# Seven-product output GEMM in the second MLP, and block 1's attention turned by TensorE, in a pooled-attention plus two-MLP kernel

## Chip, cores and metric

One core of one Trainium2 chip. The metric is the device time of one execution in microseconds (us). Before the change it is 1756.0 us, the median of three runs (1752.55 to 1757.51).

## What is computed

```python
def _attn_ref(q, k, v):                       # q, k, v: (8, 8, 576, 64)
    k_p = k.reshape(B, H, Sp, 8, D).mean(axis=3)
    v_p = v.reshape(B, H, Sp, 8, D).mean(axis=3)
    scores = scale * np.matmul(q, k_p.transpose(0, 1, 3, 2))
    scores = scores - np.max(scores, axis=-1, keepdims=True)
    attn = np.exp(scores)
    attn = attn / (np.sum(attn, axis=-1, keepdims=True) + 1e-09)
    return np.matmul(attn, v_p)

def _moe_ref(x, w_in, w_out):                 # (4608, 512) -> 2048 -> 512
    h = x @ w_in
    g = np.where(h >= 1, h, np.where(h <= -1, 0.0, (h + 1) ** 2 / 4))
    return g @ w_out

def _moe2_ref(x, w_gate, w_val, w_out):       # (4608, 512) -> 1536 -> 512
    gate = 1.0 / (1.0 + np.exp(-(x @ w_gate)))
    return (gate * (x @ w_val)) @ w_out
```

The attention's output, turned to 4608 tokens by 512, goes through the first MLP and its result through the second. All arrays are fp32.

## The kernel before

The 4608 tokens are nine blocks of 512 (`TB`). Every fp32 product of the MLPs is made of three matmuls of rounded parts: `three` (L578) multiplies high by high, high by low and low by high. So an operand has to be split first: ScalarE rounds it to its high part, VectorE subtracts that and leaves the low part (`split2`, L698; `split_to`, L704; `high_part` and `low_part`, L502 and L512).

**Attention.** `unit` (L363) does two heads of one block: load the queries, turn them, multiply with the pooled keys, exponentials and sums, turn the exponentials, multiply with the pooled values. There are 36 of them, four per block; those of block j + 1 run beside the first MLP of block j. Block 0 is turned by TensorE (`first`, L364: transposes at L384 and L447, a copy out of PSUM after each). All other blocks are turned by VectorE's stream transposes of 32 x 32 pieces: the queries at L401, loaded in pieces of 32 x 32 by eight SP transfers per unit at L395, and the exponentials at L458, which then need twelve SP transfers `aT<-aq` per unit (L464) that put the pieces in place.

**First MLP.** For each block and each of 16 column groups, `columns` (L584) makes `h<-x,win`, ScalarE and VectorE the activation and its split, and four groups of `acc<-g,wj` add up the output. The weights `w_in` and `w_out` are loaded as the first block needs them (`weight`, L527; loads at L543 and L547) and converted by ScalarE and VectorE (L551 to L565). The weights of the second MLP are loaded meanwhile, and their converted form kept in DRAM.

**Second MLP.** Block 0 is done plainly, while `prepare` (L730) builds the sums of gate and value weights that Strassen's method (in Winograd's form) wants, splits them and stores them in DRAM (`seven`, 12 tensors of 1.79 MB). Blocks 1 to 8 go in four pairs. For each pair, each of six steps `i` and for gate and value, seven products (`product`, L882) of six matmuls each take the place of eight: the 2 x 2 parts of the weights are multiplied with the inputs of two blocks and their sums (`T1` to `T4`). Their results are combined by VectorE's additions (`add`, L890) and one ScalarE copy of a bank to SBUF (L917), then `finish` (L897) makes sigmoid and product. The out GEMM is plain: `out_part` (L779) splits the activations `gs` and makes `acc<-win,g`, 144 matmuls per block, with the output weights held in SBUF; `out_rows` (L592) copies four banks out and stores them.

**What sets the order.** `Plan` (L66 to L193) is a list scheduler that runs while the program is built. Each operation has an engine, a cost and a due time (`key`); `issue` takes for the engine that is free first the operation whose data and buffers are ready, with the smallest key. Each engine then works through its list in order, and so does SP's queue of transfers. The keys around the change are:

```python
T0, S1, S2 = START, STEP1, 7.8
def due1(s): return T0 + S1 * s
def due2(j, m): return due1(NB * M1 + 2) + S2 * (j * M2 + m)
PSTEP = 11 * 2.6
PAIR0 = due2(1, 0) + 1
T0p = PAIR0 + PSTEP * MP * pr                 # start of pair pr; MP = 6 steps
T = T0p + PSTEP * i + PSTEP / 2 * n           # n: gate or value
```

PSUM has eight banks: four `acc`, two `h`, two `a`. A pair's products use `h` and `a`, its out GEMM `acc`.

Of the kernel before, what the change touches and what calls it, by code (L numbers as in the profile page):

```python
# [18 lines left out]
P = 128  # L19
# [45 lines left out]
class Plan:  # L65
# [7 lines left out]
    def op(self, eng, cost, key, fn, r=(), w=(), after=(), behind=(), nbytes=0, share=1.0, dmas=1):  # L73
# [24 lines left out]
        o.data, o.order = data, order - data  # L98
# [98 lines left out]
def pooled_attention_two_mlps(  # L197
# [46 lines left out]
    one, att, two = ExitStack(), ExitStack(), ExitStack()  # L244
# [118 lines left out]
    def unit(j, p, T):  # L363
        h0, first = 2 * p, j == 0  # L364
# [9 lines left out]
        if first:  # L374

            qs = buf_a("q", 2, [P, NT4, 2, D])
            for h in range(2):
                op(SP, 0.475, T - 20, lambda h=h: nc.sync.dma_start(
                    out=qs.t[:, :, h], in_=q[0, h0 + h, 0:TB].rearrange("(s t) d -> s t d", t=NT4)), w=[qs], nbytes=TB * D * 8)
            ptq = bank("acc")  # L380

            def transposes():
                for t in range(NT4):
                    nc.tensor.transpose(out=ptq.t[:, P * t:P * t + P],  # L384
                                        in_=qs.t[:, t].rearrange("s h d -> s (h d)"), identity=ident.t)
# [18 lines left out]
        e = buf_g(F32, (P, NT4, 2, P)) if first else e_sb  # L404
        sums = buf_a("sm", 2, [P, NT4, 2])

        scs = [bank("h" if first and p % 2 else "a") for _ in range(2)]
# [31 lines left out]
        if first:  # L439

            flat = Src(aT, lambda t: t.rearrange("c a h t j -> c (a h t j)"))
            for h in range(2):
                pt = bank("acc")

                def transposes(h=h, pt=pt):
                    for t in range(NT4):
                        nc.tensor.transpose(out=pt.t[:C].rearrange("c (s t) -> c t s", t=NT4)[:, t], in_=e.t[:, t, h, 0:C], identity=ident.t)  # L447
# [21 lines left out]
        px, x = bank("acc" if first else "a"), buf_x()  # L469

        def values():
            for t0, n, b, s0 in segs:

                cuts = sorted({t0, t0 + n} | {c for c in (-(-t0 // P) * P, (t0 + n) // P * P) if t0 < c < t0 + n})
                for lo, hi in zip(cuts, cuts[1:]):
                    for h in range(2):
                        at = aT.t[:, :, h].rearrange("c a t j -> c t a j")
                        if first:
                            rhs = flat()[:, TB * h:TB * h + TB]
# [7 lines left out]
        op(PE, 0.86 + 0.25 * (len(segs) > 1 and j % 2), T + 18 - AHEAD_PX * first, values,  # L487
           r=[aT] + [vps[b % 2, p] for _, _, b, _ in segs], w=[px], share=C / P)
        op((ACT, DVE), (0.48, 0.6), T + 19 - AHEAD_PX * first, (
# [3 lines left out]
        op(DVE, 0.6, T + 19 - AHEAD_PX * first, lambda: nc.vector.scalar_tensor_tensor(  # L493
# [175 lines left out]

    pools2 = {}  # L670

    def second_a():
        att.close()
        pools2["wa"] = two.enter_context(tc.tile_pool(name="wa", bufs=2))

    def second_b():
        one.close()
        pools2["right"] = two.enter_context(tc.tile_pool(name="two", bufs=1, side="right"))

    open_a = op("none", 0.0, 0.0, second_a, behind=att_ops)  # L680
    open_b = op("none", 0.0, 0.0, second_b, behind=one_ops)

    def late(tag, bufs, shape, dtype=F32, fifo=True):

        b = Buf(lambda: pools2["wa" if tag == "wa" else "right"], tag, bufs, shape, dtype, fifo)
        b.behind = [open_a if tag == "wa" else open_b]
# [6 lines left out]
    def buf_win(behind):  # L693
        b = Buf(win_p, "win", M1, [P, 2, TB], F32R)
# [14 lines left out]
    PSTEP = 11 * 2.6  # L709
# [55 lines left out]
    def load_seven(n, i, key):  # L765
        sl, d = buf_seven(), seven[2 * i + n]
        op2(SP, 0.475, key, lambda: nc.sync.dma_start(
            out=sl.t.rearrange("p s k f -> p (s k f)").bitcast(F32), in_=d.t), r=[d], w=[sl], nbytes=P * 2 * NMAT * HK * 4)
        return sl
# [9 lines left out]
    def out_part(gs, m, key, accs, last, ahead=5):  # L779
        g = buf_g()  # L780
        op2(ACT, 0.62, key - ahead, lambda: nc.scalar.copy(out=g.t[:, 0], in_=gs.t), r=[gs], w=[g])  # L781
        op2(DVE, 0.69, key - ahead + 1, lambda: nc.vector.tensor_tensor(  # L782
            out=g.t[:, 1], in0=gs.t, in1=g.t[:, 0].bitcast(F32), op=ALU.subtract), r=[gs, g], w=[g])
# [6 lines left out]

    def buf_gs():
        return late("gs", 12, [P, TB], fifo=False)
# [9 lines left out]
    accs = [bank("acc") for _ in range(4)]  # L802
# [167 lines left out]
```

## Time and profile before

| | us |
|---|---|
| median of three runs | 1756.0 |
| lowest, highest | 1752.55, 1757.51 |
| the profiled execution, its own time | 1755.67 |
| its span | 1753.8 |
| TensorE (PE) busy | 1723.8 (98%) |
| VectorE (DVE) busy | 1051.5 (60%) |
| ScalarE (ACT) busy | 805.7 (46%) |
| GpSimd (POOL) busy | 52.7 (3%) |

The profile is one execution. The span runs from its first to its last instruction; the time of the execution is 1.9 us longer. TensorE's granted clock was 0.995 of full speed over the span. A matmul's duration in the rows includes its way through the array, so the cost of one among many is read from the distance of two starts. Line numbers in rows are those of the kernel before; from L384 on the changed kernel's lines are five higher (`three` is L585 to L587 there), and more from L667 on.

### The profile page before, as it was taken

Reading aid. Unit: us, or ns where it says so; the run is one execution under the profiler, and the core shown is the slowest. Engines: PE = TensorE matmul, PEld = TensorE weight load, DVE = VectorE, ACT = ScalarE, POOL = GpSimd, SP = SyncE. Lnnn points to the kernel's source line nnn. Section 1 sums busy time; section 2 is a strip of 40 time slices with the busy share of each in tenths; the row PEclk is TensorE's granted clock in tenths of the full one; section 3 lists DMA queues with packets and bytes.
Section 4 is the critical chain, followed back from the end, with each engine's and each line's share of the span. In section 5 each row is a group of like instructions: output and inputs, shape, how many; then the busy total and the mean of one; then the engine's idle time right before and its main releaser. Section 6 shows DMA issues by size and latency. Waiting matters only on the chain.

```text
span 1753.8 us, 24039 instructions
## 1 busy us (share of the span) xinstructions
PE 1723.8 (98%) x9016; PEld 1393.4 (79%) x9016; DVE 1051.5 (60%) x1874; ACT 805.7 (46%) x1786; POOL 52.7 (3%) x90
## 2 busy tenths in 40 slices
PE   7899999999999999999999999999999999999998
PEld 5676777778777778777887888888888888888887
DVE  5899867677776867574646645345444644464432
ACT  5876656566665656564755332123222312141212
POOL 0000001010010101010000000000000000000000
PEclk9999999999999999999999999999999999999999
DMA  7742525243443414031415875354344433443411
GB/s 205 229 119 69 149 57 163 62 134 97 116 116 92 134 45 134 16 128 40 174 39 202 318 291 204 126 192 145 126 146 166 149 119 146 166 167 126 150 43 49
DMA packets 148532, 234.37 MB, mean 134 GB/s; under 512 B 84160, under 2 KB 104640, under 8 KB 140736
## 3 DMA queue, kind: packets, MB, share of 16 engines
q1 hardware_dynamic: 138624, 182.50, 33.1%
q0 software_dynamic: 9792, 50.34, 7.9%
q8 instruction: 71, 1.16, 0.3%
q14 instruction: 45, 0.37, 0.1%
HBM read 173.02 MB, written 50.33 MB: 127 GB/s over the span
## 4 chain that ended last, share of the span: by engine, by line
PE 92%; DMA 3%; DVE 2%; ACT 1%; SPq 0%; issue 0%; DVEq 0%; ACTq 0%
PE acc L580 13%; PE h L580 13%; PE acc L582 13%; PE acc L581 13%; PE h L582 13%; PE h L581 12%; PE a L582 4%; PE a L581 4%; PE a L580 4%; PE a L484 2%; DMA raw<-in_moe_w_out_dram 1%; PE a L413 1%; DMA kv<-in_v_dram 1%; DMA x<-in_v_dram 1%; DMA xb<-y 0%
## 5 line engine op out<-in xcount | busy, mean ns | idle before, releaser
L580 PE MATMUL h<-x,win 128*128 128x512 f32 x576 | 231.2, 401 | 1.0 <-ACT win L505 1.0
L580 PE MATMUL acc<-g,wj 128*128 128x512 f32 x576 | 228.7, 397 | 1.2 <-ACT g L505 1.2
L582 PE MATMUL acc<-g,wj 128*128 128x512 f32 x576 | 225.4, 391 | 3.5 <-DVE wj L514 3.5
L582 PE MATMUL h<-x,win 128*128 128x512 f32 x576 | 225.7, 392 | 1.3 <-DVE win L514 1.3
L581 PE MATMUL acc<-g,wj 128*128 128x512 f32 x576 | 225.6, 392 | 1.0 <-DVE g L514 1.0
L581 PE MATMUL h<-x,win 128*128 128x512 f32 x576 | 225.5, 391 | 0.0
L781 ACT CAST g<-gs 128x512 fp32r<-128x512 f32 x108 | 66.8, 622 | 319.2 <-PE acc L582 200.4
L645 ACT ACTIVATE t<-h,half 128x512 f32<-128x512 f32 x144 | 99.2, 689 | 186.9 <-PE h L582 186.9
L582 PE MATMUL acc<-win,g 128*128 128x512 f32 x432 | 168.2, 389 | 2.1 <-DVE g L782 2.1
L580 PE MATMUL acc<-win,g 128*128 128x512 f32 x432 | 168.2, 389 | 0.0
L581 PE MATMUL acc<-win,g 128*128 128x512 f32 x432 | 168.1, 389 | 0.0
L782 DVE TENSOR_TENSOR g<-gs,g 128x512 fp32r<-128x512 f32 x108 | 74.1, 690 | 135.2 <-ACT g L781 135.0
L649 DVE SCALAR_TENSOR_TENSOR t<-t,h 128x512 f32<-128x512 f32 x144 | 97.3, 676 | 90.9 <-ACT t L647 90.8
L580 PEld LDWEIGHTS h<-x,win 128*128 128x128 f32 x576 | 108.7, 189 | 35.7 <-issue 9.7
L582 PEld LDWEIGHTS acc<-g,wj 128*128 128x128 f32 x576 | 108.4, 188 | 28.4 <-DVE wj L514 5.4
L580 PEld LDWEIGHTS acc<-g,wj 128*128 128x128 f32 x576 | 108.2, 188 | 27.8 <-ACT g L505 1.7
L582 PEld LDWEIGHTS h<-x,win 128*128 128x128 f32 x576 | 108.7, 189 | 25.9 <-DVE win L514 2.5
L581 PEld LDWEIGHTS acc<-g,wj 128*128 128x128 f32 x576 | 108.3, 188 | 23.2 <-DVE g L514 1.6
L581 PEld LDWEIGHTS h<-x,win 128*128 128x128 f32 x576 | 108.8, 189 | 21.1
L514 DVE TENSOR_TENSOR wj<-wout_f,wj 128x512 fp32r<-128x512 f32 x144 | 99.0, 688 | 33.3 <-ACT wj L505 33.0
L514 DVE TENSOR_TENSOR g<-t,g 128x512 fp32r<-128x512 f32 x144 | 98.8, 686 | 33.6 <-ACT g L505 33.1
L505 ACT CAST g<-t 128x512 fp32r<-128x512 f32 x144 | 89.1, 619 | 52.5 <-DVE t L649 50.1
(212 smaller groups left out, 3231.1 us busy)
## 6 DMA issues: line engine op xcount, KB each, us to landing
wa<-seven SPq DMA_DIRECT2D x32, 1792.0 KB
wb<-seven SPq DMA_DIRECT2D x16, 1792.0 KB
seven<-wa POOLq DMA_DIRECT2D x8, 1792.0 KB, 7.4
y<-raw SPq DMA_DIRECT2D x18, 512.0 KB
w<-f POOLq DMA_DIRECT2D x36, 256.0 KB, 2.5
out_dram<-raw SPq DMA_DIRECT2D x18, 512.0 KB
win<-in_moe_w_in_dram SPq DMA_DIRECT2D x16, 512.0 KB
raw<-in_moe_w_out_dram SPq DMA_DIRECT2D x16, 512.0 KB
```

The lines of the kernel that those rows point to most:

```text
L413: nc.tensor.matmul(out=scs[h].t[r0 % P:r0 % P + D, r0 // P * C:r0 // P * C + C], lhsT=qT.t[D * h:D * h + D, r0:r0 + D], rhs=kts[b % 2, p]. ...
L484: nc.tensor.matmul(out=px.t[D * h:D * h + D, lo:hi], lhsT=vps[b % 2, p].t[:, h], rhs=rhs, start=True, stop=True)
L505: ACT: (0.52, lambda: nc.scalar.copy(out=dst.t[:, 0], in_=src())),
L514: op(engs, [0.6 if e == DVE else 1.23 for e in engs], key, [lambda e=e: by[e].tensor_tensor(out=dst.t[:, 1], in0=src(), in1=dst.t[:, 0].bi ...
L580: nc.tensor.matmul(out=o, lhsT=wh, rhs=xh, start=start, stop=False, skip_group_check=more)
L581: nc.tensor.matmul(out=o, lhsT=wh, rhs=xl, start=False, stop=False, skip_group_check=more)
L582: nc.tensor.matmul(out=o, lhsT=wl, rhs=xh, start=False, stop=stop, skip_group_check=more)
L645: op(ACT, 0.69, Tg, lambda t=t, hps=hps: nc.scalar.activation(out=t.t, in_=hps.t, func=AF.Relu, bias=half.t, scale=0.5), r=[hps, half], w=[t])
L649: op(DVE, 0.69, Tg + 2, lambda t=t, hps=hps: nc.vector.scalar_tensor_tensor(out=t.t, in0=t.t, scalar=1.0, in1=hps.t, op0=ALU.min, op1=ALU. ...
L781: op2(ACT, 0.62, key - ahead, lambda: nc.scalar.copy(out=g.t[:, 0], in_=gs.t), r=[gs], w=[g])
L782: op2(DVE, 0.69, key - ahead + 1, lambda: nc.vector.tensor_tensor(out=g.t[:, 1], in0=gs.t, in1=g.t[:, 0].bitcast(F32), op=ALU.subtract), r ...
```

## The change

It has four parts.

1. **Block 1 is turned by TensorE too** (`first = j <= 1`). Its queries come in 16 transfers of 256-byte pieces and not 32 of 128-byte pieces, 16 transposes and 32 transposes of exponentials are added on TensorE with banks `a`, twelve copies out of PSUM follow (eleven on ScalarE, one on VectorE by the order), and twelve stream transposes and 48 transfers `aT<-aq` go.

2. **The out GEMM of a pair goes by seven products** (`out_pair`): seven products of six steps of two banks of three matmuls, 252 for 288. `prepare_out` builds and splits the sums of output weights in pair 0 and stores them in DRAM (42 tiles `seven_o`, by POOL); each product loads them again (`wo`, five buffers). The activations' sums are made in place by VectorE (24 per pair), each product's own split follows (42 per pair, 24 before). The output comes out transposed: `store` turns it by VectorE and stores 256-byte pieces, and the last part of the last pair goes through eight transposes of TensorE (`store_rows`).

3. **Gate and value products in another order**, with sums made in PSUM: ScalarE copies a finished bank into the next one (`to_bank`), and the next product adds to it. Weights come one product at a time (256 KB, `ws`, nine buffers) and not seven at a time (1.79 MB, three buffers).

4. **Input sums kept in DRAM** (`input_sums`): those of pairs 1 to 3 are made during the pair before, stored and loaded again; pair 0 makes its own as before.

Per engine the order counts 6912 matmuls of 512 columns by three parts after the change and 7056 before.

```diff
-        h0, first = 2 * p, j == 0
+        h0, first = 2 * p, j <= 1
...
+            where = "acc" if j == 0 else "a"
+            ptq = bank(where)
...
-                        out=pt.t[:C].rearrange("c (s t) -> c t s", t=NT4)[:, t], in_=e.t[:, t, h, 0:C], identity=ident.t)
+                        out=pt.t[:C, P * t:P * t + P], in_=e.t[:, t, h, 0:C], identity=ident.t)
...
-    PSTEP = 11 * 2.6
+    PSTEP = 10.5 * 2.6
...
-    def load_seven(n, i, key):
-        sl, d = buf_seven(), seven[2 * i + n]
+    def load_seven(n, i, mat, key):
+        w, d = late("ws", 9, [P, 2, HK], F32R), seven[2 * i + n]
...
+        for k in range(NMAT):
+            src, n = (a, (0, 2, 3)[k]) if k < 3 else (sm, k - 3)
+            w = buf_wo()
...
+            op2(PL, 1.0, key + 2 + k, lambda w=w, k=k: nc.gpsimd.dma_start(
+                out=seven_o[i][k].t, in_=w.t.rearrange("p s f -> p (s f)").bitcast(F32)), r=[w], w=[seven_o[i][k]], nbytes=P * 2 * HK * 4)
...
+        def product(n, mat, o, start, what):
+            chain = []
+            for i in range(MP):
+                key = K0 + KP * (n + i / MP)
+                w, g = late("ws", 9, [P, 2, HK], F32R) if last and n and i % 3 else buf_wo(), buf_g() if i % 2 else late("g2", 3, [P, 2, TB], F32R)
+                op2(SP, 0.475, key - 20, lambda w=w, i=i: nc.sync.dma_start(
+                    out=w.t.rearrange("p s f -> p (s f)").bitcast(F32), in_=seven_o[i][mat].t),
+                    r=[seven_o[i][mat]], w=[w], nbytes=P * 2 * HK * 4)
+                h1, h2 = hs[i]
+                src, b = what(key - 32, h1, h2)
+                split_to(key - 30, lambda src=src, b=b: src.t[:, b], lambda g=g: g.t[:, 0], lambda g=g: g.t[:, 1], 0.69, src, g)
+
+                def mm(w=w, g=g, i=i):
+                    for e in range(2):
+                        es = slice(e * P, e * P + P)
+                        three(o[e].t, w.t[:, 0, es], w.t[:, 1, es], g.t[:, 0], g.t[:, 1],
+                              start and i == 0, i == MP - 1, not start)
...
+        X, Y = [bank("acc", True) for _ in range(2)], [bank("acc", True) for _ in range(2)]
+        product(0, 0, X, True, lambda k, h1, h2: (h1, 0))
+        s1 = o_buf()
+        to_sbuf(key(1) - 30, X, s1)
...
+        if pr == 0:
...
+        else:
+            order = (("B11", B11), ("T1", T1), ("T2", T2), ("B21", B21), ("T3", T3), ("B22", B22), ("T4", T4))
+            for n, (name, x) in enumerate(order):
+                for kt in range(2):
...
+                    op2(SP, 0.475, key - AHX, lambda x=x, kt=kt, d=d, r0=r0: nc.sync.dma_start(
+                        out=x[kt].t[:, 1].bitcast(F32), in_=d.t[r0 * P:(r0 + 1) * P, :]), r=[d], w=[x[kt]], nbytes=P * TB * 4)
+                    x_split(x[kt], key)
...
+            if pr + 1 < NPR and i in (2, 4):
+                input_sums(pr + 1, i // 2 - 1, T0p + PSTEP * (i + SUM0), plan.ops[-1])
...
                 product(0, A, 0, B11, True)
-                op(ACT, 0.6, T + H * 1, lambda s1=s1, A=A: nc.scalar.copy(out=s1.t, in_=A.t), r=[A], w=[s1])
-                product(1, Bk, 4, T2, True)
-                add(T + H * 2, u2, Bk, s1)
-                product(2, Ck, 5, T3, True)
-                add(T + H * 3, u3, Ck, u2)
-                product(3, Dk, 3, T1, True)
-                finish(T + H * 4, (1, 1), Dk, u3)
-                product(4, A, 1, B21, False)
-                finish(T + H * 5, (0, 0), A, None)
-                product(5, Ck, 2, T4, False)
-                finish(T + H * 6, (1, 0), Ck, u2)
-                product(6, Dk, 6, B22, False)
-                finish(T + H * 7, (0, 1), Dk, u2)
+                to_bank(T + H * 1, A, Bk)
+                product(1, Dk, 3, T1, True)
+                op2(ACT, 0.6, T + H * 2 + 0.6, lambda u5=u5, Dk=Dk: nc.scalar.copy(out=u5.t, in_=Dk.t), r=[Dk], w=[u5])
+                product(2, Bk, 4, T2, False)
+                to_bank(T + H * 3, Bk, Ck)
+                op2(ACT, 0.6, T + H * 3 + 1, lambda u2=u2, Bk=Bk: nc.scalar.copy(out=u2.t, in_=Bk.t), r=[Bk], w=[u2])
+                product(3, A, 1, B21, False)
+                finish(T + H * 4, (0, 0), A, None)
+                product(4, Ck, 5, T3, False)
+                finish(T + H * 5, (1, 1), Ck, u5)
+                product(5, Dk, 6, B22, False)
+                finish(T + H * 6, (0, 1), Dk, u2)
+                product(6, Ck, 2, T4, False)
+                finish(T + H * 7, (1, 0), Ck, None)
```

SP's queue while block 0 is in the first MLP and block 1's attention runs, before (`q` are query pieces, `aT<-aq` the exponentials' pieces, `raw` a weight load):

```order
L313 DMA kv<-in_k_dram 72x2x512
L395 DMA q<-in_q_dram 32x2x32
L395 DMA q<-in_q_dram 32x14x32
L464 DMA aT<-aq 32x256
L547 DMA raw<-in_moe_w_out_dram 128x1024
L464 DMA aT<-aq 32x256
L464 DMA aT<-aq 8x256
L464 DMA aT<-aq 32x256 x2
```

The same place after:

```order
L380 DMA q<-in_q_dram 16x4x64
L380 DMA q<-in_q_dram 112x4x64
L552 DMA raw<-in_moe_w_out_dram 128x1024
L313 DMA kv<-in_v_dram 72x2x512
L313 DMA kv<-in_k_dram 72x2x512
L313 DMA kv<-in_v_dram 72x2x512
L552 DMA raw<-in_moe_w_out_dram 128x1024 x2
L400 DMA q<-in_q_dram 32x4x32
```

The transfers `aT<-aq` that stood among the weight loads are gone, and the queries come in larger pieces.

TensorE in a pair after the change (`h` and `a` are banks, `x` inputs, `ws` weights): the end of the product on bank a_12264, the next product on h_12245, and the first matmul on h_12301, a bank into which ScalarE copies a_12264.

```order
L587 MATMUL a_12264<-x_11326,ws_12188 128x512
L585 MATMUL h_12245<-x_11337,ws_12197 128x512
L586 MATMUL h_12245<-x_11337,ws_12197 128x512
L587 MATMUL h_12245<-x_11337,ws_12197 128x512
L585 MATMUL h_12245<-x_11342,ws_12197 128x512
L586 MATMUL h_12245<-x_11342,ws_12197 128x512
L587 MATMUL h_12245<-x_11342,ws_12197 128x512
L585 MATMUL h_12301<-x_11353,ws_12207 128x512
```

ScalarE at that place (`g` are splits for the out GEMM):

```order
L1159 ACTIVATE f_12240<-f_12240 128x512
L1159 ACTIVATE f_12254<-h_12209 128x512
L1170 COPY a_12264<-h_12245 128x512
L722 CAST g_12277<-win_11289 128x512
L1178 COPY u_12288<-a_12266 128x512
L1170 COPY h_12301<-a_12264 128x512
L1181 COPY u_12304<-a_12264 128x512
```

The six matmuls on h_12245 are all that lies between the product that is copied and the first matmul on the copy; on ScalarE the copy into h_12301 stands behind a split and the copy u_12288.

ScalarE in a pair before the change had copies to SBUF only (L917), between splits (L781) and sigmoids (L903):

```order
L917 COPY f_12526<-h_12507 128x512
L903 ACTIVATE t_12552<-t_12552 128x512
L903 ACTIVATE t_12561<-h_12507 128x512
L903 ACTIVATE f_12566<-f_12566 128x512
L781 CAST g_12578<-gs_11801 128x512
L903 ACTIVATE f_12590<-f_12590 128x512
L917 COPY f_12600<-h_12581 128x512
```

Nothing on TensorE waited for a ScalarE copy there but by way of VectorE's additions; now products wait for it directly.

## Rows read from the trace of the kernel before

**Rows 1.** The page, busy time, share of the span and instructions

```profile
span 1753.8 us, 24039 instructions
...
PE 1723.8 (98%) x9016; PEld 1393.4 (79%) x9016; DVE 1051.5 (60%) x1874; ACT 805.7 (46%) x1786; POOL 52.7 (3%) x90
```

**Rows 2.** The page, the chain that ended last, share by engine

```profile
PE 92%; DMA 3%; DVE 2%; ACT 1%; SPq 0%; issue 0%; DVEq 0%; ACTq 0%
```

**Rows 3.** Windows: us, busy us of PE, PEld, DVE, ACT, POOL; PEclk, DMA share, GB/s

```profile
1000.00:1700.00 700.00, 700.00 (x3090) 579.83 (x3089) 335.40 (x506) 182.93 (x308) 1.60 (x3) 1.00 0.43 157
1700.00:1754.00 54.00, 49.25 (x218) 40.46 (x216) 16.33 (x24) 13.64 (x23) 0.00 (x0) 0.98 0.10 39
```

**Rows 4.** Windows of 10 us from 40 to 180 us, and their sum

```profile
50.00:60.00 10.00, 6.98 (x51) 5.08 (x50) 9.19 (x19) 7.43 (x26) 0.00 (x0) 0.83 1.07 329
...
sum 140.00, PE 128.34 PEld 96.86 DVE 127.59 ACT 102.73 POOL 0.00; mean PE 9.17 PEld 6.92 DVE 9.11 ACT 7.34 POOL 0.00
```

**Rows 5.** The chain from 30 to 100 us: start, us, what

```profile
61.08 9.34 DMA raw<-in_moe_w_out_dram
...
80.01 1.20 PE a L484 x12
```

**Rows 6.** Timeline of PE near 1730 us: start, us, what

```profile
1724.83 0.39 PE L581 MATMUL acc<-win,g 128*128 128x512 f32 x1
...
1737.52 0.39 PE L580 MATMUL acc<-win,g 128*128 128x512 f32 x1
```

**Rows 7.** ScalarE's groups by form: busy us, mean ns | idle before

```profile
L781 ACT CAST g<-gs 128x512 fp32r<-128x512 f32 x108 | 66.8, 622 | 319.2 <-PE acc L582 200.4 <-DVE gs L910 88.1 <-DVE gs L823 30.4
...
L917 ACT COPY f<-h 128x512 f32<-128x512 f32 x48 | 28.2, 587 | 66.2 <-PE h L582 65.0
```

**Rows 8.** VectorE's groups by form

```profile
L458 DVE STREAM_TRANSPOSE aq<-e_sb 128x384 f32<-128x384 f32 x64 | 33.3, 556 | 0.0
L891 DVE TENSOR_TENSOR u<-h,u 128x512 f32<-128x512 f32 x48 | 33.2, 692 | 26.6 <-PE h L582 26.3
...
L401 DVE STREAM_TRANSPOSE qT<-q 128x512 f32<-128x512 f32 x32 | 22.5, 703 | 5.1 <-DMA q<-in_q_dram 5.1
```

**Rows 9.** Timeline from 1102 us, end of a product and its reader

```profile
1104.22 0.39 PE L582 MATMUL h<-x,wa 128*128 128x512 f32 x1
...
1104.64 0.69 DVE L891 TENSOR_TENSOR u<-h,u 128x512 f32<-128x512 f32 x1 [0.60 <-PE h L582]
```

**Rows 10.** The page, DMA issues: KB each, us to landing

```profile
w<-f POOLq DMA_DIRECT2D x36, 256.0 KB, 2.5
```

**Rows 11.** Timeline of the end

```profile
1748.86 0.39 PE L582 MATMUL acc<-win,g 128*128 128x512 f32 x1
```

**Rows 12.** Timeline of PE from 24 us, block 0's transposes

```profile
24.22 0.66 PE L384 MATMUL acc<-ident,q 128*128 128x128 f32 x4
24.71 0.60 PE L447 MATMUL acc<-ident,g 128*72 128x128 f32 x4
...
28.74 1.07 PE L447 MATMUL acc<-ident,g 128*72 128x128 f32 x8
29.64 0.49 PE L353 MATMUL acc<-x,ident 72*72 72x128 f32 x3
```

**Rows 13.** Timeline of SP's queue from 300 us

```profile
309.45 7.58 SPq L464 DMA_DIRECT2D aT<-aq  x12
```

**Rows 14.** DMA queue from 1040 to 1100 us: packets, MB, share

```profile
q1 hardware_dynamic: 1348, 11.94, 54.9%
```

**Rows 15.** DMA queue from 760 to 800 us

```profile
q1 hardware_dynamic: 1328, 0.98, 9.1%
```

**Rows 16.** DMA queue from 225 to 250 us

```profile
q1 hardware_dynamic: 2981, 1.24, 21.5%
```

More of the change, by code (lines that the diff above doesn't have):

```diff
@@ L97, in op @@
         data.discard(o)
-        o.data, o.order = data, order - data
+        o.data, o.order = data, order - data - {o}
         o.issued = False
@@ L241, in pooled_attention_two_mlps @@
           "a": (ctx.enter_context(tc.tile_pool(name="ps_a", bufs=2, space=PSUM)), 2)}
-    one, att, two = ExitStack(), ExitStack(), ExitStack()
+    one, att, two, zero, zero_a = (ExitStack() for _ in range(5))
     edge = ctx.enter_context(tc.tile_pool(name="edge", bufs=1, side="right"))
@@ L402, in unit @@
                r=[qs], w=[qT])
-        e = buf_g(F32, (P, NT4, 2, P)) if first else e_sb
+        e = buf_g(F32, (P, NT4, 2, P)) if j == 0 else e_sb
         sums = buf_a("sm", 2, [P, NT4, 2])
-        scs = [bank("h" if first and p % 2 else "a") for _ in range(2)]
+        scs = [bank("h" if j == 0 and p % 2 else "a") for _ in range(2)]
         def scores():
@@ L467, in unit @@
                         r=[aq], w=[aT], nbytes=n * 1024)
-        px, x = bank("acc" if first else "a"), buf_x()
+        px, x = bank("acc" if j == 0 else "a"), buf_x()
         def values():
             for t0, n, b, s0 in segs:
-                cuts = sorted({t0, t0 + n} | {c for c in (-(-t0 // P) * P, (t0 + n) // P * P) if t0 < c < t0 + n})
+                cuts = sorted({t0, t0 + n} | {c for c in (-(-t0 // P) * P, (t0 + n) // P * P) if t0 < c < t0 + n and not first})
                 for lo, hi in zip(cuts, cuts[1:]):
@@ L801, in pooled_attention_two_mlps @@
         x_split(xs[c], due1(NB * M1 - 2))
-    accs = [bank("acc") for _ in range(4)]
+    accs, wb_slots = [bank("acc") for _ in range(4)], []
     for i in range(MP):
         slots = [prepare(n, i, due2(0, 2 * i) - 6 + 2.6 * n) for n in range(2)]
+        wb_slots += [x for x, _ in slots]
         T = due2(0, 2 * i)
@@ L875, in pooled_attention_two_mlps, with buf_h @@
+        def buf_h(i):
+            if (MP * pr + i) % 8 < 2:
+                return late("gs", 4, [P, 2, TB], fifo=False)
+            return buf_win([], F32, False)
+        hs = [[buf_h(i) for _ in range(2)] for i in range(MP)]
         for i in range(MP):
+            if pr + 1 < NPR and i in (2, 4):
+                input_sums(pr + 1, i // 2 - 1, T0p + PSTEP * (i + SUM0), plan.ops[-1])
             sig = {}
@@ L879, in pooled_attention_two_mlps, with product @@
                 H = PSTEP / 14
[L880 to L882 removed]
+                def product(pos, o, mat, xx, start):
+                    w = load_seven(n, i, mat, T + H * pos - 30)
                     def mm():
```

298 lines of the change are left out of this document (231 added, 67 removed).

## The prediction

> **What bounds the kernel now.** I read the busy times of the engines first [rows 1], then the chain that ended last [rows 2], then the windows [rows 3, 4]. The reader should see that TensorE is the bound almost everywhere: it is busy for 1723.8 of 1753.8 us, 92% of the chain is its own work, and from 1000 to 1700 us, where the pairs of MLP2 run, it has no idle time in 700 us, while VectorE is busy for 335 us of them and ScalarE for 183. There a matmul less is time less, and work on the two other engines is free as long as nobody waits for it. Two stretches differ. From 40 to 180 us TensorE is busy for 128.3 of 140 us and VectorE for 127.6 [rows 4]; the chain there goes through a 9.34 us wait for a weight load [rows 5]. The last 54 us leave TensorE idle for 4.75 us, most of it after the last matmul.
>
> The cadence of the matmuls that go is read where they run back to back: start 1724.83, 56 starts later 1737.52 [rows 6], so 12.69 / 56 = 0.2266 us each. The duration of 0.39 us in those rows is latency, not cost.
>
> **The out GEMM by seven products: the gain.** Before, a pair of blocks takes 2 x 12 x 4 x 3 = 288 matmuls; after, 7 products x 6 x 2 x 3 = 252. Over four pairs 144 go, all 512 columns wide, at full clock, on an engine without idle time: 144 x 0.2266 = **-32.6 us**. The gate and value products keep their 504 matmuls per pair in another order.
>
> What it adds lies on VectorE and ScalarE. In a full pair (738 to 792 matmuls, 167 to 180 us) the order has some 140 ScalarE and 145 VectorE instructions. At about 0.6 us (a copy of a bank: 0.587, [rows 7]) and 0.69 us (an addition, [rows 8]) that is 84 and 100 us: 50% and 60% of the stage. I cost it at nothing in the mean, since the cover is another engine's matmuls; the places where the cover is thin follow.
>
> **Tight links.** ScalarE's copy of one bank into the next stands between two products (96 such copies), a VectorE addition between others (48). By the order, in 37 of the copies and 18 of the additions only six matmuls lie between the last one of the product that is read and the first one that waits. From the start of the last matmul to the start of its reader it is 0.42 us [rows 9]; the copy takes 0.587 [rows 7]; with another 0.06 us until TensorE can go on (an estimate), that is 1.07 us, and the seven starts span 7 x 0.2266 = 1.59. About half a microsecond is spare, so an idle ScalarE costs nothing. No row shows a copy from bank to bank; the nearest bounds are the 0.587 us of bank to SBUF and the 0.69 us of VectorE's addition from a bank [rows 8], and both fit. I take 0.
>
> **Transitions between pairs.** Pairs 1 to 3 now load 14 tiles and split them where the previous pair's products end, and the out GEMM's tail must cover that. Before, TensorE shows no idle time at these places [rows 3]. Bounds: 0, and 3 us each (14 loads of 256 KB are 3.7 MB; at the 22.6 GB/s per engine worked out below, 16 engines take 10.1 us for them, against 8 us of matmuls by the order, and the first split follows). Nearest is no idle time, but with 14 + 14 splits bunched up I take 1 us each: **+3.0**, bounds 0 and +9. After block 0 the first weight tiles can only come once the old pool is free: 18 matmuls, 4.1 us, cover a transfer of 256 KB that lands in 2.5 us [rows 10] behind its issue; **+0.4**, bounds 0 and 1. In pair 0 ScalarE's splits for the out weights wait for a POOL store five tiles back, 2.5 us to landing [rows 10]; by the order other work of ScalarE lies between those five, so I take 0, with a bound of +5 (42 splits, each 0.1 us late, an estimate) if bank copies queue behind them.
>
> **The end.** Now the last matmul starts 4.9 us before the end [rows 11]. After: reader's latency 0.42, one or two additions 0.69 to 1.38, four or eight transposes 0.5 to 1.0 (next paragraph), 0.42 again, a copy 0.59, a landing of 256 KB 2.5: 5.1 to 6.3 us, and up to 0.5 for the issue. **+1.0**, bounds +0.2 and +1.9.
>
> **Block 1 turned by TensorE.** Added: 16 + 32 transposes. Four for the queries take 24.71 - 24.22 = 0.49 us, eight of exponentials 29.64 - 28.74 = 0.90 us [rows 12]: 16 x 0.1225 + 32 x 0.1125 = **+5.6 us** of TensorE. The eight value matmuls that go are worth at most 0.8 (twelve in 1.2 us, [rows 5]); since they split the same columns, I count 0. Removed from VectorE: 4 x 0.703 + 8 x 0.556 [rows 8], less one copy of 0.69 that it takes on: 6.6 us. ScalarE gets eleven copies, 6.5 us, in a stretch where it is busy for 73% [rows 4]. On SP 48 transfers from SBUF to SBUF go, at 7.58 us for twelve [rows 13]: 30 us of that queue, in which weight loads stand behind them, and 16 query loads of 128-byte pieces.
>
> Idle TensorE time in reach is 140 - 128.3 = 11.7 us [rows 4]. Its neighbour at 91% loses 6.6 us. Bounds of what comes back: 0 and 11.7. Nearest is what VectorE loses, less a little for waits that are the DMA's: I take 5.0. Net **+0.6**, bounds +5.6 and -6.1. If VectorE's relief is used up, the next late thing is the weight load.
>
> **Sum.** -32.6 + 0.6 + 3.0 + 0.4 + 1.0 = -27.6. The profiled execution took 1755.7, so 1728.1; it lies 0.3 below the median of the runs, so the forecast is **1728** us. All low ends together (-32.6 - 6.1 + 0.2 = -38.5) give 1717.5; all high ends (-32.6 + 5.6 + 9 + 1 + 1.9 + 5 = -10.1) 1746.
>
> **Rivals.** First, nothing waits at the transitions and block 1's relief returns all the idle time: the low end, 1717.5. For it: 700 us without a gap now. Against: the weight loads on the early chain [rows 5] stay as large as they are.
>
> Second, the DMA engines become the bound of the pairs. Per pair the changed kernel moves 84 weight tiles (22.0 MB in 1-KB rows) and some 21 MB more in rows of 2 KB mostly, 43 MB in 171 us (252 GB/s), where the pair stage shows 157 GB/s [rows 3]. Prices: 1348 packets of 8.9 KB took 54.9% of 16 engines over 60 us, 391 ns each, which is 22.6 GB/s per engine; 1328 of 738 bytes took 9.1% over 40 us, 44 ns; 2981 of 416 bytes 21.5% over 25 us, 29 ns [rows 14 to 16]. A line through the ends is 11 ns and 43 ns per 1000 bytes, so 55 ns for 1 KB and 99 for 2 KB: (21500 x 55 + 10250 x 99) / 16 = 137 us, with the 256-byte pieces of the output 142 us, 83% of the stage. The bound is crossed if packets cost 1.21 times that; at 1.25 times, three full pairs lose 6 us each: 1728 + 18 = 1746; I put this case at 1745. For it: large loads are cut to 256 KB. Against: engines ran at 1.07 of their time and 329 GB/s for ten microseconds [rows 4].
>
> The Trainium skill's page "DMA: Bandwidth & Descriptors", section "Measured", speaks against this change: it wants transfers of 1 MB and more for three quarters of the peak, with 341 GB/s for 1 MB and 138 for 64 KB, and the change cuts loads of 1.8 MB to 256 KB. Between these two rates the 43 MB of a pair would take 126 to 312 us (estimates from that page) against a stage of 171, so by the middle of it the kernel would get slower rather than faster. No row here shows many transfers of 256 KB in flight at once; by that rule it is the second rival, or worse, that comes.
>
> Third, and slower: the copies come late. ScalarE works in order, so a copy that finds two splits ahead of it (2 x 0.62, [rows 7]) starts 1.24 us late, 0.72 past the spare time; on all 55 tight links that is 39.6 us and the time is 1728 + 40 = 1768. It decides from a mean lateness of 0.52 + 27.6 / 55 = 1.02 us. For it: ScalarE goes from 26% to 50% busy. Against: at half load one operation ahead costs 0.62 at most, hardly past the spare time, and what stands ahead of the copies in the order's rows (a split and a copy in the place shown) has its data earlier than they.
>
> **Chances and range.** What a measurement can tell from no change is 0.3%, 5.3 us: 1750.7 to 1761.3. Forecast, 1721 to 1735: 0.55. First rival: 0.14. Second: 0.25, of which 0.20 ends below 1750.7 and 0.05 within 0.3%. Third: 0.06, slower. The range of 1716 to 1746 leaves out a twentieth below and about 0.15 above. Faster 0.89, same 0.05, slower 0.06.
>
> **What would show it.** Right: 512-column matmuls down from 7056 to 6912; windows in the pair stage with TensorE still full; VectorE's share in 40 to 180 us falling with TensorE's idle time no larger than 12 us; DMA share of the pairs near 0.8. Wrong: gaps of TensorE before the accumulating products with the bank copy as releaser (third rival); gaps with the weight tiles' loads as releaser and a DMA share near 1 (second); a stretch 0 to 180 us that ends later by over 5 us (block 1's turning gives nothing back).

## The result and the profile after

The changed kernel takes 1730.37 us, the median of four runs (1726.36 to 1731.51), beside 1756.01 for the kernel before; the ratio is 0.9855 with a 95% interval of 0.9841 to 0.9868. In four later runs it took 1729.71 (ratio 0.9857, 0.9838 to 0.9875). The forecast was 1728 with a range of 1716 to 1746. The execution profiled below took 1730.95.

The page of the changed kernel, its span, its busy times and its chain by engine:

```profile
span 1729.1 us, 25598 instructions
...
PE 1697.3 (98%) x8912; PEld 1370.0 (79%) x8912; DVE 1109.0 (64%) x2006; ACT 956.9 (55%) x2074; POOL 76.1 (4%) x134
...
PE 87%; DMA 5%; DVE 3%; issue 2%; ACT 2%; SPq 1%; POOL 1%; POOLq 0%; DVEq 0%; ACTq 0%
```

Against [rows 1, 2] TensorE is busy for 26.5 us less, and its share is the same. ScalarE is busy for 151 us more, VectorE for 58. The windows that answer to [rows 3], and the sum of those of 10 us from 40 to 180 us that answers to [rows 4]:

```profile
1000.00:1700.00 700.00, 696.45 (x3063) 573.85 (x3062) 396.29 (x644) 332.19 (x593) 23.71 (x44) 1.00 0.83 261
1700.00:1730.00 30.00, 23.26 (x104) 18.45 (x102) 14.41 (x22) 8.49 (x14) 0.00 (x0) 0.94 0.31 87
```

The sum over the early windows:

```profile
sum 140.00, PE 133.76 PEld 103.14 DVE 128.34 ACT 110.75 POOL 1.66; mean PE 9.55 PEld 7.37 DVE 9.17 ACT 7.91 POOL 0.12
```

The pair stage has small gaps now, 3.55 us in 700, and the DMA engines are busy for 0.83 of the stage. Early, TensorE's idle time (the window less its busy time) fell from 11.7 to 6.2 us, but VectorE is as busy as before.

To see where the 24.7 us of span went I use three points: the start of the second MLP, its last 512-column matmul, and the end. The first of them before the change, on TensorE's timeline:

```profile
929.17 0.39 PE L580 MATMUL h<-x,wa 128*128 128x512 f32 x1
```

And both after it:

```profile
925.87 0.39 PE L585 MATMUL h<-x,wa 128*128 128x512 f32 x1
...
1722.31 0.39 PE L587 MATMUL acc<-g,ws 128*128 128x512 f32 x1
```

Before, the second MLP takes 1748.86 [rows 11] - 929.17 = 819.69 us for 3600 matmuls, after 1722.31 - 925.87 = 796.44 for 3456. The 144 that went are worth 144 x 0.2267 = 32.64, so 9.4 us came back as waits. The tail grew from 1753.8 - 1748.86 = 4.94 to 6.79.

| term | forecast | this execution | a second one of the same kernel |
|---|---|---|---|
| 144 matmuls | -32.6 | -32.6 | -32.6 |
| start of the second MLP (block 1's turning) | +0.6 | -3.3 | +1.6 |
| waits within the second MLP | +3.4 | +9.4 | +6.6 |
| tail | +1.0 | +1.85 | +1.8 |
| sum against the span before | -27.6 | -24.7 | -22.6 |

(The second execution has a span of 1731.2; its second MLP runs from 930.81 to 1724.46.) The 9.4 us have two parts, found as what the distances between neighbouring matmul starts have above 0.2267 us ("by starts" below). Block 0's plain part, up to 1030 us, lost 6.2 us where the kernel before lost 3.9; the pairs lost 7.0 where it lost nothing. In the second execution the two parts are 4.4 and 6.1. What TensorE waited for from 900 us on, in the first:

```profile
PE acc L587 <- DVE g L799: 2.3, 1, 2.3
PE a L585 <- ACT a L1170: 1.1, 2, 0.9
PE h L585 <- DVE t L1147: 0.9, 1, 0.9
PE a L585 <- ACT u L1178: 0.8, 1, 0.8
PE acc L585 <- ACT g L722: 0.7, 1, 0.7
PE h L585 <- ACT h L1170: 0.5, 1, 0.5
PE acc L585 <- ACT g L798: 0.5, 1, 0.5
PE h L939 <- DVE raw L915: 0.5, 2, 0.3
PE acc L585 <- DMA wo<-seven_o: 0.3, 1, 0.3
```

A wait costs 0.16 us more than its row says, since a matmul's shown duration of 0.39 reaches past its cadence of 0.227. The three transitions between pairs (at 1160, 1322 and 1495 us) lost 1.1, 1.2 and 0.4 us, in the second execution 0.2, 0.5 and 0.3. In block 0 the wait of 2.3 us is for a split that VectorE made behind a weight sum, and the sum had waited for its load:

```profile
943.93 0.42 DVE L768 TENSOR_TENSOR raw<-f,wa 128x256 f32<-128x256 f32 x1 [1.75 <-DMA wa<-w]
```

It was followed by a stretch at half clock, in this window at the 1.2 GHz level throughout:

```profile
945.00:950.00 5.00, 4.06 (x10) 3.19 (x11) 5.00 (x10) 2.82 (x6) 0.00 (x0) 0.50 0.49 204
```

The kernel before waited about as long for the same split, and its clock in the same window stayed at 1.00:

```profile
PE acc L582 <- DVE g L782: 2.1, 1, 2.1
...
945.00:950.00 5.00, 2.91 (x12) 1.89 (x11) 5.00 (x11) 2.73 (x6) 0.43 (x1) 1.00 0.99 394
```

### The profile page after: what moved, and what is told of

Its sections match the earlier page's. It is cut to its first block, busy times and chain, and to the rows that moved or that the text cites. A ratio compares the mean times of both kernels' runs of the same rounds, so it can differ in the third digit from the quotient of the medians.

```text
span 1729.1 us, 25598 instructions
## 1 busy us (share of the span) xinstructions
PE 1697.3 (98%) x8912; PEld 1370.0 (79%) x8912; DVE 1109.0 (64%) x2006; ACT 956.9 (55%) x2074; POOL 76.1 (4%) x134
## 4 chain that ended last, share of the span: by engine, by line
PE 87%; DMA 5%; DVE 3%; issue 2%; ACT 2%; SPq 1%; POOL 1%; POOLq 0%; DVEq 0%; ACTq 0%
PE h L585 12%; PE acc L585 12%; PE h L587 12%; PE h L586 12%; PE acc L587 12%; PE acc L586 12%; PE a L585 4%; PE a L587 4%; PE a L586 4%; PE a L489 2%; PE a L418 1%; DMA seven_o<-wo 1%; POOL seven_o L877 1%; DMA q<-in_q_dram 1%; DMA x<-y 1%
## 5 line engine op out<-in xcount | busy, mean ns | idle before, releaser
L723 DVE TENSOR_TENSOR g<-win,g 128x512 fp32r<-128x512 f32 x126 | 85.9, 688 | 108.0 <-ACT g L722 107.7
L722 ACT CAST g<-win 128x512 fp32r<-128x512 f32 x126 | 78.2, 624 | 94.2 <-PE acc L587 80.4
L585 PE MATMUL acc<-g,wo 128*128 128x512 f32 x288 | 112.4, 390 | 1.0 <-ACT g L722 0.7
L585 PE MATMUL h<-x,ws 128*128 128x512 f32 x288 | 112.3, 390 | 0.5 <-ACT h L1170 0.5
L587 PE MATMUL acc<-g,wo 128*128 128x512 f32 x288 | 112.1, 389 | 0.0
```

Of the source, the lines that this page charges most:

```text
L585: nc.tensor.matmul(out=o, lhsT=wh, rhs=xh, start=start, stop=False, skip_group_check=more)
L587: nc.tensor.matmul(out=o, lhsT=wl, rhs=xh, start=False, stop=stop, skip_group_check=more)
L722: op2(ACT, cost, key, lambda: nc.scalar.copy(out=out_hi(), in_=val()), r=[src, b], w=[b])
L723: op2(DVE, cost, key + 0.5, lambda: nc.vector.tensor_tensor(out=out_lo(), in0=val(), in1=out_hi().bitcast(F32), op=ALU.subtract), r=[src, ...
```

## The experiments

My theory after the first result was the table: the gain is the deleted matmuls, block 1's turning is worth about 3 us, the links have half a microsecond to spare, and the DMA engines have a fifth. Its rivals: block 1's turning is worth nothing, or costs; the copies bind nowhere or bind already; the DMA engines have less room. In the expectations "the changed kernel" is the one profiled above.

### Block 1's turning, undone and alone

```diff
-        h0, first = 2 * p, j <= 1
+        h0, first = 2 * p, j <= 0
```

> The changed kernel with block 1's queries and exponentials turned by VectorE again; everything else stays. In the trace of the changed kernel the 61st to 661st matmul of the first MLP start earlier than before the change, by 3.3 us from 210 us on, although 48 transposes were added. If that is what block 1's turning on TensorE is worth, this kernel is 3 us slower than the changed one: 1733 to 1734, and from 210 us on its matmuls start where those of the kernel before did. If the forecast's price is right (5.6 us of transposes against 5.0 of idle time that comes back), it is 0.6 us faster: 1730. If TensorE's transposes only cost, it is 5 us faster: 1725.

The other kernel is the one before with the changed `unit` put in, and one line of `Plan` that the change has too (`order - data - {o}`).

> The kernel before with block 1's turning on TensorE alone. Same question from the other side, with the old second MLP behind it: 1752.7 if the turning is worth 3.3 us, 1756.6 by the forecast's price, 1761 if the transposes only cost. Together with the kernel with VectorE's turning it also tells whether the two halves of the change add up (then this one lies as far below the kernel before as that one lies above the changed kernel).

Measured: undone 1733.69 us (ratio to the kernel before 0.9877, 0.9857 to 0.9896), alone 1759.38 (1.0022, 1.0009 to 1.0036). Undoing it costs 3.3 us by the medians, with intervals that overlap, and 1733 to 1734 was expected if the turning is worth 3 us; adding it alone costs 3.9, between the forecast's price (1756.6) and bare cost (1761). The two contradict each other if the halves of the change add up, so neither figure is the price of the turning.

The traces say why. Up to the second MLP the orders on all engines are row for row those of the changed kernel, or, with VectorE's turning, of the kernel before. So up to there all kernels of this study but the two that touch block 2's transfers are samples of two programs. With TensorE's turning ten of them start the second MLP at 925.9 to 932.8 us, 928.6 in the mean; with VectorE's two start it at 927.2 and 929.2, 928.2 in the mean. That fits the forecast's +0.6, but with two samples on one side and a spread of 7 us on the other it can't be told from a gain or a loss of 2 us. The 3.3 us of my first table were one execution's luck. The two blocks show more than the sum: with TensorE's turning block 0's last matmul of the first MLP starts at 171.4 us in the mean, with VectorE's at 174.2; from there to block 1's last it is 99.5 us (97.8 to 102.1) against 96.3 both times; and behind that all take the same 658 us. What differs between executions lies in two places: waits near 60 us and the clock there, and in block 1 a wait near 200 us (below) and the clock after it. The window from 60 to 70 us of the changed kernel's first execution:

```profile
60.00:70.00 10.00, 8.70 (x68) 6.94 (x72) 8.20 (x16) 9.23 (x19) 0.00 (x0) 1.00 0.55 170
```

The same window of the kernel with a copy of every fourth load (below), whose order is the same there:

```profile
60.00:70.00 10.00, 7.68 (x59) 6.33 (x57) 5.00 (x12) 4.83 (x10) 0.00 (x0) 0.66 0.65 173
```

In the second, TensorE waited 2.3 us for a load of block 1's keys, from 60.7 us on, the granted clock was 0.66, and the first block's last matmul started at 174.9 us; in the first it started at 169.8. In the kernel with the turning alone the excess over the kernel before is 1.1 us at the start of the second MLP, 2.3 in block 0's second MLP (a wait of 3.94 us in place of 2.25, by starts) and nothing later.

### Copies made later

```diff
-                    op(ACT, 0.6, key, lambda: nc.scalar.copy(out=dst.t, in_=src.t), r=[src], w=[dst])
+                    def copies():
+                        for _ in range(2):
+                            nc.scalar.copy(out=dst.t, in_=src.t)
+                    op(ACT, 0.6, key, copies, r=[src], w=[dst])
```

> The changed kernel, but ScalarE makes each of the 96 copies from one product bank into the next twice in a row; the order and everything else stay, and the second copy writes the same values. Products that add to the bank wait for the second one, so each such link becomes about 0.57 us longer. By the forecast's working a tight link (six matmuls between) has 1.59 us for 1.07 us of work, so 0.5 us to spare: then 37 tight copies lose some 0.05 to 0.1 us each, the other copies nothing, and ScalarE's 54 us more cost little elsewhere; 1733 to 1738. If the spare time were less than 0.3 us as run, each tight link would lose 0.3 us or more and the time would be over 1741. If the copies bind nowhere, 1730.

With `range(3)`:

> The same with each copy made three times, 1.14 us longer per link, which is past the spare time of the tight links by 0.6 us and within that of the links with twelve matmuls between (1.9 us). Theory of the third rival: 37 x 0.6 = 22 us and a few more for queues behind ScalarE, which is then busy for 62% of the pairs: 1752 to 1762. If the copies bind nowhere (their products would have more cover than the order shows), under 1740.

Measured: twice 1738.55 us (ratio 0.9904, 0.9873 to 0.9934), thrice 1761.95 (1.0042, 1.0029 to 1.0055). The waits of TensorE in the pairs with three copies, longest groups (L1172 is the repeated copy):

```profile
PE h L585 <- ACT h L1172: 14.2, 28, 0.6
PE a L585 <- ACT a L1172: 6.7, 11, 1.1
```

39 waits, where the order has 37 tight copies. A typical one is a distance of 0.66 us above the cadence for 1.14 us of delay, so 0.48 us was spare; with two copies the same places lose mostly 0.06 for 0.57, which leaves 0.51. Behind each such wait the next matmul starts another 0.11 us late. Thrice came out at the upper end of what was expected, twice 0.5 us above it. The third rival's price was right: half a microsecond is to spare at each tight link, and past it every tight link pays. The copy itself takes less than I bounded:

```profile
L1170 ACT COPY h<-a 128x512 f32<-128x512 f32 x48 | 27.4, 571 | 31.4 <-PE a L587 29.7 <-DVE o L867 0.8 <-DVE win L889 0.8
...
L1178 ACT COPY u<-a 128x512 f32<-128x512 f32 x48 | 28.3, 589 | 39.7 <-PE a L587 39.7
```

from bank to bank 571 ns, against 589 from bank to SBUF in the same kernel and 587 before [rows 7]. The Trainium skill's page "ScalarE: Activation LUTs", section "Step-by-step: what each stage is for", says that ScalarE writes faster to PSUM than to SBUF; the trace agrees, by 16 to 18 ns.

### More bytes for the DMA engines

```diff
+        def load():
+            nc.sync.dma_start(out=w.t.bitcast(F32), in_=rows)
+            turns[0] += 1
+            if turns[0] % 4 == 0:
+                extra = dram.tile([P, 2, HK], F32, name=f"extra{turns[0]}")
+                nc.sync.dma_start(out=extra, in_=rows)
```

> The changed kernel, and behind every fourth load of a weight tile SP issues a copy of the same 256 KB (rows of 1 KB) from DRAM to a DRAM tile that nobody reads: 84 copies in all, 21 per pair, 13% more bytes read. The DMA engines' share in 1200 to 1300 us was 0.79 and a packet of 1 KB took 56 ns, as the forecast's line has it. If the second rival's price is right, the share rises to about 0.9 (a copy within DRAM may cost up to twice a load) and nothing waits but in pair 0, where the engines were at 1.05 already: 1730 to 1735.

With `% 2`:

> The same behind every second load: 168 copies, 42 per pair, 26% more bytes. The forecast put the point from which the DMA engines bind the pairs at 1.21 times their work. Then the share reaches 1 and each pair loses some microseconds: 1745 to 1765, with waits of TensorE for weight tiles. If the pairs have room still (prefetch of nine tiles hides it), below 1738.

Measured: 1743.57 us (ratio 0.993, 0.9903 to 0.9957) and 1762.07 (1.0043, 1.0028 to 1.0058). The first expectation missed by 9 us; the second time lies in its range. The windows of pair 0 and of the other pairs, first of the changed kernel (last three columns: granted clock, DMA share, GB/s):

```profile
1030.00:1200.00 170.00, 167.81 (x736) 137.41 (x735) 100.53 (x186) 89.69 (x177) 22.65 (x42) 1.00 0.96 336
1200.00:1700.00 500.00, 498.64 (x2196) 411.62 (x2195) 282.46 (x438) 233.10 (x402) 0.00 (x0) 1.00 0.80 237
```

With a copy of every fourth load:

```profile
1030.00:1200.00 170.00, 162.35 (x704) 132.68 (x703) 98.31 (x183) 85.21 (x168) 22.62 (x42) 0.99 1.04 373
1200.00:1700.00 500.00, 495.06 (x2173) 408.67 (x2172) 271.13 (x419) 227.22 (x394) 0.00 (x0) 1.00 0.86 264
```

With a copy of every second one:

```profile
1030.00:1200.00 170.00, 155.36 (x645) 122.75 (x645) 94.92 (x178) 80.16 (x160) 22.62 (x42) 0.97 1.07 392
1200.00:1700.00 500.00, 491.39 (x2146) 404.17 (x2145) 259.45 (x400) 221.65 (x385) 0.00 (x0) 0.99 0.91 292
```

TensorE's idle time in pair 0 goes from 2.2 over 7.7 to 14.6 us, and in the 500 us after it from 1.4 over 4.9 to 8.6, where the share is only 0.80 to 0.91. So more transfers cost time, nearer than I put the second rival: waits begin well before the mean share reaches 1, and pair 0 has no room at all. That the transfers come in bunches is the likely reason, not a tested one. A second is SP's queue: each copy also takes some 0.6 us of it to issue, ahead of the next loads, and no run separates the two. The packets cost what the forecast's line said. In 1200 to 1300 us of the changed kernel (the first line is the DMA engines' share in tenths, in slices of 2.5 us):

```profile
DMA  7589687999898898567566676999578878789947
...
q1 hardware_dynamic: 22766, 23.99, 79.1%
```

that is 0.791 x 16 x 100 us / 22766 = 55.6 ns for 1054 bytes; the line gives 56. Against [rows 14], with 391 ns for 8.9 KB, a byte costs about a fifth more.

### Input sums made again

```diff
-        if pr == 0:
+        if pr >= 0:
...
-            if pr + 1 < NPR and i in (2, 4):
+            if False:
```

> The changed kernel, but the input sums of pairs 1 to 3 are made by VectorE at the start of the pair, as pair 0 does, and not kept in DRAM. Each transition gets 8 additions of 0.69 us, 5.5 us of VectorE, in a stretch where it is busy for 17 of 20 us, and 4 to 6 loads less. The transitions of the changed kernel lose 2.7 us of TensorE's time in all. Theory: VectorE's splits bound the transitions, so they lose some 2 us more each, 1736. Rival: the loads bound them, then it gets no slower and the gaps shrink, 1728 to 1730.

Measured: 1737.09 us (ratio 0.9896, 0.9876 to 0.9916). By starts its pairs lose 12.7 us and not 7.0, and the added gaps lie mostly at the transitions (1153 to 1163, 1326, 1500 to 1520 us). The theory's time holds: sums in DRAM are worth some 6 us, in traffic that the DMA engines still carry there. That VectorE is what binds the transitions is not shown: the largest wait, 2.8 us by starts at 1326 us, is for an output weight's tile, and most of the others are for ScalarE.

### Block 0's first split

```diff
-                r=[sl, a21] + ([sm] if o else []), w=[sm])
+                r=[sl, a21] + ([sm] if o else []), w=[sm], behind=first_split if (i, n) == (1, 1) else [])
```

> The changed kernel, but one VectorE group in block 0's second MLP (the weight sums of the second step's value half) may be issued only after the first split for the out GEMM. In the changed kernel the first split stood behind such a sum that waited 1.75 us for its load at 942 us; TensorE stood for 2.5 us and went at half clock for the next 8 matmuls and part of others, 2.5 us more lost than in the kernel before. If the split in front of the sums removes both, the time falls by 3 to 4.5 us, to 1726 to 1727, and the granted clock of 945 to 955 us stays at 1.00. If the stall only moves to the weight sums (their product waits instead), the time stays at 1730. The rest of the order changes too, so single gaps of the pairs may come out otherwise by a microsecond or two.

Measured: 1734.72 us (ratio 0.9879, 0.9864 to 0.9894), no gain. Its own place did improve and kept full clock, but ten microseconds on there is a new wait of 1.73 us for a split:

```profile
945.00:950.00 5.00, 4.34 (x18) 2.85 (x17) 5.00 (x12) 2.79 (x6) 0.00 (x0) 1.00 0.98 367
955.00:960.00 5.00, 3.43 (x15) 2.25 (x13) 5.00 (x12) 1.33 (x2) 0.53 (x1) 1.00 0.66 275
```

VectorE is full in both, and the late split waited 4.5 us for a VectorE product that stood behind more weight sums, so the stall moved to the next thing that VectorE does. Pair 0 has a new wait too, 2.3 us at 1106 us for a weight tile. The second MLP as a whole is 1.6 us shorter than in the changed kernel's first execution and 1.2 longer than in its second.

### Block 2's transfers, the spread sums, and all together

The first of these kernels is the changed one again.

> The changed kernel itself, unchanged, in more rounds and on the same chip as the three variants that follow. In the traces so far a program's first MLP ends by up to 7 us earlier or later with the same order: the seven kernels with block 1 turned by TensorE start the second MLP at 925.9 to 932.8 us, late ones with a stretch of half clock at 60 to 70 us. So its median should lie between 1729 and 1735, with single runs from 1726 to 1738.

Then, in `unit`, with a list of each unit's transfers `aT<-aq`:

```diff
-                op(SP, 0.475, T - 20, lambda f=f: load_q(f), w=[qs], nbytes=TB * 256, dmas=len(segs))
+                op(SP, 0.475, T - 20, lambda f=f: load_q(f), w=[qs], nbytes=TB * 256, dmas=len(segs),
+                   behind=pieces.get((j, p - 2), []) if j == 2 else [])
```

> The changed kernel, but block 2's query loads may be issued only after the transfers of exponential pieces of the unit two before. In the changed kernel SP issued eight query loads from 179.0 to 187.6 us while the pieces were ready at 183.6; they went from 187.7 to 196.4, and TensorE waited for them for 2.1 us at 195.7 (1.6 to 3.0 in the other kernels with block 1 on TensorE). If that queue is where the gain of block 1's turning was lost, the wait goes and the second MLP starts 2 to 3 us earlier; the median falls by 2 to 3 us against the changed kernel. If VectorE, busy for 10 of 10 us before, is what is late, the wait turns into one for VectorE and the time stays.

```diff
-        prepare_out(i, PAIR0 + PSTEP * (0.2 + 0.6 * i))
+        prepare_out(i, PAIR0 + PSTEP * (0.2 + 0.9 * i))
```

> The changed kernel, but the output weights' sums of pair 0 are made over five and a half steps and not four (due every 0.9 of a step, before 0.6). The DMA engines were at 1.05 from 1040 to 1120 us, and TensorE lost 2.2 us there in three gaps; with 13% and 26% more bytes the same stretch (1030 to 1200) lost 7.7 and 14.6 us. If the DMA engines make these gaps, spreading the 42 stores takes 1 to 2 us off. If ScalarE's order makes them, the time stays; if the out GEMM then comes too early for the last sums, it waits at some 1138 us.

> The split before the weight sums in block 0 (tried above: its own place lost 1.6 us less and kept full clock), the pieces before the queries, and the spread sums, all three. If their places are independent and each is worth what its place lost: 1.6 + 2.5 + 1 = 5 us below the changed kernel, which would beat both kernels. If the order shifts elsewhere give it back, no more than 2 us.

Measured against the kernel before: the changed kernel again 1729.71 us, 0.9857 (0.9838 to 0.9875), as expected but for one run of 1723.55 below the range; pieces before queries 1726.91 us, 0.9844 (0.9828 to 0.9860); sums spread 1736.39, 0.9899 (0.9882 to 0.9916); all three 1734.83, 0.9886 (0.9872 to 0.9900).

Block 1's turning ran into the queue of block 2's pieces. SP's timeline in the changed kernel: eight query loads ahead of the pieces that had been ready since 183.6.

```profile
179.02 8.54 SPq L400 DMA_DIRECT2D q<-in_q_dram  x8
187.67 2.98 SPq L469 DMA_DIRECT2D aT<-aq  x3
```

and the wait of TensorE for them, from 180 to 210 us:

```profile
PE a L489 <- DMA aT<-aq: 2.1, 1, 2.1
```

With the edit that wait is gone. From the first block's last matmul to the second's it is 96.8 us, in the changed kernel 98.4 and 101.9 (in the second execution the wait was 3.0 and the clock fell after it), before the change 96.3. The second MLP of this one execution starts at 928.7 us and not earlier, as was expected, since it lost its time near 60 us (block 0's last matmul at 174.2). The median is 2.8 us below the changed kernel on the same chip, as expected in size; the intervals overlap, so it is the best median of the study and not a proven gain.

Spreading the sums failed (1 to 2 us less was expected, some 7 more came), and shows how full pair 0 is. From 1040 to 1140 us the gaps did go, but then the sums met the next pair's input loads:

```profile
1040.00:1140.00 100.00, 100.00 (x443) 82.65 (x442) 58.11 (x117) 50.62 (x107) 20.53 (x39) 1.00 1.00 354
1140.00:1160.00 20.00, 15.31 (x53) 10.86 (x52) 14.74 (x24) 11.46 (x20) 0.54 (x1) 0.83 1.03 373
```

4.7 us idle and a lower clock, in waits for splits of inputs that land late. The kernel with all three edits has the same hole (5.6 us by starts from 1150 to 1170), and the early split gained nothing in it either (block 0 lost 5.7 us). It was expected 5 us below the changed kernel and came out 5 above.

## Why the prediction was right, and where its steps were off

**The gain.** 144 matmuls at the cadence of 0.2267: right, the count is 3456 against 3600 in the second MLP and the cadence between waits is the same. "TensorE still full in the pair stage" was nearly so, 696.5 of 700 us.

**Block 1's turning.** The net of +0.6 is not contradicted: 928.6 against 928.2 us in the mean of the traces, too few to fix it to better than 2 us. Its reason was half right. Idle time from 40 to 180 us fell by 5.4 us in the first execution (by 3 to 6 in the ten), where the forecast had 5.0, but the sign that I named for it, VectorE's share falling, did not come there (128.3 against 127.6 us; 123.8 to 127.8 in the others): VectorE probably used the freed time for the work that came next. And what I named as next late, the weight load, was the wrong one. It was block 2's exponential pieces behind query loads in SP's queue, which took some 3 us back (99.5 us for block 1 against 96.3), about what block 0 had gained.

**Transitions.** Forecast 1 us each, measured 1.1, 1.2 and 0.4, and 0.2, 0.5 and 0.3 in the second execution: 2.8 and 1.0 for 3.0. The first weight tiles after block 0 showed no wait.

**Waits left out.** This is the step that was off. I put pair 0 at 0 with a bound of 5 for ScalarE's queue, because a split of an output weight waits only for a store that lands in 2.5 us [rows 10], with other work of ScalarE between. In pair 0 these stores took 5.7 us to land, as the page of the changed kernel shows; ScalarE waited for them 11 times from 1036 to 1120 us, and a bank copy came late behind one such split:

```profile
seven_o<-wo POOLq DMA_DIRECT2D x42, 256.0 KB, 5.7
...
ACT wo L722 <- DMA seven_o<-wo: 12.4, 11, 2.6
...
1044.69 0.41 ACT L722 CAST wo<-o 128x256 fp32r<-128x256 f32 x1 [1.38 <-DMA seven_o<-wo]
1045.00 0.58 ACT L1170 COPY h<-a 128x512 f32<-128x512 f32 x1
```

That copy cost TensorE 0.7 us, and an addition at 1096 us behind the same kind of split on VectorE 1.0; pair 0 lost 2.4 us up to 1150 us, 2.6 in the second execution. With the sums spread, the gaps up to 1140 us went. A split in the last out GEMM cost another 1.0 in both executions, and waits for output weights' tiles 0.6 and 1.3. Block 0's second MLP, also left at 0, cost 2.3 us more than before in the first execution and 0.4 in the second, mostly by the half clock after a wait that was there before too. The sum of waits was 6.6 to 9.4 where the forecast had 3.4. In the first execution the early start of the second MLP, which was luck, hid more than half of the difference.

**The end.** +1.0 with a bound of +1.9; measured +1.85, as both additions and seven of the eight transposes lie one behind the other.

**Rivals.** The first did not come: there are waits at every transition. The second did not decide, and its share of 83% came out as 0.80 in the full pairs, but 13% more traffic costs over 10 us, so its 1.21 (171 / 142 is 1.20) was too generous; the mean share hides how full single stretches are. The third did not decide either, though its sign, a gap with the bank copy as releaser, came three times (0.7, 1.1 and 0.3 us by starts); its spare time was 0.48 to 0.51 for 0.52. The 0.06 us in its sum stands in no row by itself; the whole link, 1.59 less the spare time, came out as 1.1 us for 1.07. The rule on large transfers of the Trainium skill's page "DMA: Bandwidth & Descriptors", section "Measured", did not come true as a time: with loads and stores of 256 KB for the most part, many at once, pair 0 moved 381 GB/s from 1040 to 1120 us.

```profile
1040.00:1120.00 80.00, 78.62 (x344) 63.88 (x343) 50.14 (x104) 42.11 (x91) 21.20 (x40) 1.00 1.04 381
```

Left open: what block 1's turning is worth to better than 4 us, since medians with the other half of the change and without it have opposite signs, why one execution waits for block 1's keys near 60 us and the next does not, and what the new order of the products and the smaller weight loads cost by themselves, since no run has them with the plain out GEMM.

## What to carry to other kernels

On an engine that is 98% busy, count its instructions at their cadence and then look for the links: here the saving came as counted, and what was given back lay in the few places where another engine's answer has less than one operation of slack. Price the room of a queue or of the DMA engines by the fullest stretch, not by the mean of the stage. A term of a few microseconds in a start-up phase can't be read from one trace each; compare several executions with the same order.

## What the runs showed that I had not expected

A wait of 2 to 3 us on TensorE can cost twice: in several places the granted clock fell in it or behind it (0.50 in 945 to 950 us, 0.66 in 60 to 70 us, 0.83 in 1140 to 1160 us), while the kernel before waited 2.1 us at the same split and kept 1.00. Whether it falls differed between executions with nearly the same wait: at block 0's split the second execution of the changed kernel waited 2.18 us by starts and then went at half clock, and the kernel with two copies waited 2.15 and kept full clock. Copies of a bank into another by ScalarE are no dearer than copies to SBUF, 571 against 587 to 593 ns.
